# An RWKV block with its MLP on one core: both units of round 0's second part treated together

## The chip, the cores and the metric

The kernel runs on one core of a Trainium2 chip. The core has five engines with instruction queues of their own, which meet only at semaphores: TensorE (PE in the profile; PEld are its weight loads), VectorE (DVE), ScalarE (ACT), GpSimd (POOL) and SyncE (SP, which here only issues DMAs). The metric is the device time of one execution in microseconds (us); lower is better. The kernel before took 469.12 us as the median of 3 runs (468.19 to 469.22).

## The reference

The inputs r, k, v and w have 4 batches, 8 heads, 768 steps and 48 numbers for each head and step; u has 48 for each head. For each batch and head a state of 48 x 48 is carried along the steps, and its result goes through a normalization and a two-layer MLP (384 to 1536 to 384):

```python
for t in range(S):
    cur = np.einsum('bhd,bhe->bhde', u[None] * kt, vt)
    y[:, :, t] = np.einsum('bhd,bhde->bhe', rt, state + cur)
    state = wt[:, :, :, None] * state + np.einsum('bhd,bhe->bhde', kt, vt)
# x: y as (batch, step, head * 48)
xn = (x - mu) / np.sqrt(var + 1e-06) * g_ln
out = x + np.maximum(xn @ w_ch1, 0.0) @ w_ch2
```

## The kernel before, in words

**Rounds, parts and units.** The work is cut into 8 rounds: 4 batches, each in two halves of 384 steps. A round holds all 8 heads, as two units of 4 heads (two pairs each); its 384 steps are three tiles of 128. Round 0 alone is cut further, into a first part of one tile and a second part of two tiles (`parts_of_round`), so that matmuls can begin early.

**One part** (`front`, line 1688). r, k and w are loaded, four steps to a row. Products inside these groups of four are made on VectorE, POOL and ACT (`inner`, tiles `nat_*`, `pad_*`, `rk`, `vals`). PE turns the padded k and r so that steps become columns (`turn`; tiles `k`, `r`, `k_ps`, `r_ps`); `totals` multiplies decays over 4, 8, 16 and 32 steps (`tot`, `decay`). Then come four levels, 2 to 5 (blocks of 4 to 32 steps):

- `quads` (line 806): PE makes the products of r and k between neighbouring blocks, for each unit 16 matmuls per tile of 128 steps (`a<-r,k`; 60, 56, 48 and 32 rows at levels 2, 3, 4 and 5).
- `grow` (line 840): VectorE multiplies k, and then r, in place by the decay of the neighbouring block (`k<-k,tot`, `r<-r,tot`), so that the next level can use them. It must wait for that unit's `quads` of the same level, and the next level's `quads` wait for it.
- `keep` and `keep_last`: masked copies on VectorE (level 4 also as four copies on ACT) and copies on ACT move the products from PSUM into the matrix A.

`inner_by_tile` sends the values inside the groups of four through DRAM into the tile `va`, and `place_own` copies them into A with a mask. `turn_k` turns k back (`kn_ps`). `states` (line 953) makes k times v on PE (`a<-v,k`), and its `scan` on VectorE runs the state through the half tiles: one operation for each pair and step, and, where no state comes from an earlier round, a plain copy for the first (`s<-a`). `inside` multiplies A by v, a tiny POOL operation (`token`) separates it from `outputs`, which adds r times the states (`a<-s,r`). The result is copied into `x`.

**Levels of the second part.** In the second part of round 0 (two tiles) each level's `quads` and `grow` are issued for one unit at a time: the list `apart` in `front` (line 1723) holds two entries, `[0]` and `[1]`. In the first part and in all later rounds it has one entry with both.

**MLP and the rest.** `normalize`, `turn_x`, `first_product` and `mlp` are the normalization and the MLP. Its weights arrive as raw words (`raw`), which ACT, VectorE and POOL make into floats (`convert`: `held`, `rest` with a sign step, a shift `w<-w`, a join `w<-w,held`). Round 0 uses plain fp32 matmuls; from round 1 on the first product uses operands cut into parts.

**What sets the order.** Nothing is left to a scheduler at run time. Every step is given to a `Plan` with a cost, the keys that it reads and writes and the engines that could run it. The method `order` walks through the long hand-out list `ORDER` (line 76), in which a number is a step and a multiple of 10000 on top of it picks the second or third of its engines; so `ORDER` sets the place of each step in its engine's queue, and for many steps the engine. Where the plan's own clock expects PE to wait for more than 0.35 us, `order` also puts in filler matmuls on zeros (`idle<-nought`), in blocks of 128 columns. A POOL operation that shares a port with VectorE is also made to wait for the VectorE operations issued before it.

```python
op = ops[entry % 10000]
e = list(op.costs)[entry // 10000]
```

Of the kernel before, what the change touches and what calls it, by code (L numbers as in the profile page):

```python
# [18 lines left out]
ALU = mybir.AluOpType  # L19
# [44 lines left out]
class Plan:  # L64
# [294 lines left out]
def kernel(  # L359
# [614 lines left out]
    def states(q, part):  # L974
# [25 lines left out]
        def scan():  # L1000
# [23 lines left out]
            count=32 * nc,  # L1024
        )
        plan.add(
            "DVE", 0.01 + 0.174 * NP * len(steps), scan, r=[kv_, (f"decay{rnd}", c0)] + sofar,
            w=[(s_, c0)] + ([last_] if last_ else []), new=[("last", last_)] if last_ else [],
            pri=urgent(part, 22),
        )  # L1030
# [794 lines left out]
```

## Time and profile before

| what | value |
|---|---|
| median of 3 runs | 469.12 us (468.19 to 469.22) |
| the profiled execution, its own time | 468.5 us |
| its span, first to last instruction | 466.7 us |
| PE busy, filler included | 458.0 us (98%) |
| of it filler on zeros | 27.94 us, all in the first 50 us |
| VectorE / ACT / POOL busy | 353.2 / 263.8 / 137.7 us |
| mean granted TensorE clock | 0.998 |

Nearly every instruction is recorded by one helper, so all have line 47; they are told apart by the tiles that they write and read. A row of the instruction list reads: start, duration of the row, engine, operation, output<-inputs, shapes, how often; in brackets the idle time of the engine ahead of it and what ended it. An engine's neighbouring instructions overlap by some hundredths of a microsecond, so the time that one takes from its queue is the distance between two starts. One fp32 matmul of the program shows as two in the trace, since the array takes such operands in two passes.

### The profile page before, as it was taken

How to read it: one execution, taken by the hardware profiler on the slowest of the kernel's cores; microseconds unless marked ns; L12 is line 12 of the kernel's file. 1: busy time of each engine (PE TensorE's matmuls, PEld its weight loads, DVE VectorE, ACT ScalarE, POOL GpSimd, SP SyncE). 2: the span in 40 equal slices, each digit the busy share in tenths (PEclk: the TensorE clock that was granted, in tenths of full speed). 3: DMA queues.
4: the chain of work that ended last, by engine and by line, in shares of the span. 5: the costliest groups of instructions: out<-in, count | busy, mean ns of one | idle time of the engine just before them, and what ended most of it. 6: DMA issues, size and time to landing. Idle time of an engine off the chain costs nothing.

```text
span 466.7 us, 17460 instructions
## 1 busy us (share of the span) xinstructions
PE 458.0 (98%) x7442; PEld 399.7 (86%) x7442; DVE 353.2 (76%) x742; ACT 263.8 (57%) x608; POOL 137.7 (30%) x141
## 2 busy tenths in 40 slices
PE   8999999999999999999999999999999999999996
PEld 5677989766999666989776899999999999999996
DVE  8999999999997768897879887976733535525535
ACT  4697889754765322665621677855555456444440
POOL 4137013332451242353443240221013122321030
PEclk9999999999999999999999999999999999999999
DMA  7987775776658505745630545302222232142011
GB/s 208 277 199 210 205 156 137 233 196 156 174 150 185 111 28 136 166 138 145 157 61 5 86 124 129 111 30 70 84 62 67 76 103 67 37 136 67 35 51 51
DMA packets 105501, 56.23 MB, mean 120 GB/s; under 512 B 61904, under 2 KB 102352, under 8 KB 105424
## 3 DMA queue, kind: packets, MB, share of 16 engines
q1 hardware_dynamic: 105152, 54.92, 45.1%
q8 instruction: 58, 0.95, 0.9%
q10 hardware_dynamic: 272, 0.20, 0.1%
q14 instruction: 19, 0.16, 0.1%
HBM read 45.27 MB, written 7.47 MB: 113 GB/s over the span
## 4 chain that ended last, share of the span: by engine, by line
PE 84%; DVE 10%; POOL 2%; issue 2%; SPq 1%; DMA 1%; DVEq 0%; POOLq 0%
PE h_ps L47 28%; PE a L47 26%; PE o L47 15%; PE o_2P L47 4%; PE o_2D L47 2%; PE k_ps L47 2%; PE r_ps L47 2%; PE kn_ps L47 2%; PE xT_ps L47 2%; DVE nat_k L47 1%; DVE s L47 1%; DVE A L47 1%; SPq L47 1%; DVE vals L47 1%; DMA nat_k<-in_k_dram 1%
## 5 line engine op out<-in xcount | busy, mean ns | idle before, releaser
L47 ACT ACTIVATE h<-h_ps 128x384 f32<-128x384 f32 (+2 forms) x108 | 47.8, 456 | 49.6 <-PE h_ps L47 48.9
L47 PE MATMUL o<-ffn,h 128*128 128x384 f32 x216 | 74.7, 492 | 0.0
L47 DVE SCALAR_TENSOR_TENSOR hD<-hH,hL 128x384 fp32r<-128x384 f32 x60 | 36.3, 616 | 37.1 <-POOL hL L47 16.0
L47 POOL TENSOR_TENSOR hL<-h,hH 128x384 fp32r<-128x384 f32 x28 | 30.1, 1081 | 102.7 <-PE a L47 27.7
L47 ACT ACTIVATE h_ps<-h_ps 128x384 f32<-128x384 f32 x84 | 39.7, 481 | 34.5 <-PE h_ps L47 33.5
L47 PEld LDWEIGHTS o<-ffn,h 128*128 128x128 f32 x216 | 39.2, 190 | 23.1
L47 PEld LDWEIGHTS a<-r,k 48*56 48x56 f32 (+3 forms) x3072 | 39.7, 122 | 10.5 <-issue 4.9
L47 PE MATMUL h_ps<-xd,d 128*128 128x384 f32 x204 | 47.1, 335 | 0.0
L47 PE MATMUL a<-r,k 48*56 48x32 f32 (+3 forms) x3072 | 44.1, 208 | 0.6 <-issue 0.2
L47 PE MATMUL h_ps<-xhl,wl 128*128 128x384 f32 x180 | 40.4, 334 | 0.0
L47 DVE TENSOR_TENSOR r<-r,tot 112x768 f32<-112x768 f32 (+1 forms) x40 | 32.2, 808 | 10.0 <-PE a L47 10.0
L47 PE MATMUL h_ps<-xhl,wh 128*128 128x384 f32 x180 | 39.1, 326 | 0.0
L47 ACT ACTIVATE hH<-h 128x384 fp32r<-128x384 f32 x60 | 29.7, 518 | 11.6 <-PE a L47 7.8
L47 DVE TENSOR_TENSOR k<-k,tot 112x768 f32<-112x768 f32 (+1 forms) x40 | 31.6, 790 | 5.5 <-PE a L47 5.4
L47 PEld LDWEIGHTS h_ps<-xd,d 128*128 128x128 f32 x204 | 34.0, 189 | 0.5
L47 DVE TENSOR_TENSOR hL<-h,hH 128x384 fp32r<-128x384 f32 x32 | 17.9, 568 | 20.0 <-PE a L47 9.5
L47 PEld LDWEIGHTS h_ps<-xhl,wh 128*128 128x128 f32 x180 | 30.8, 189 | 0.0
L47 ACT COPY A<-a 32x384 f32<-32x384 f32 (+5 forms) x56 | 23.5, 421 | 12.4 <-PE a L47 9.8
L47 PEld LDWEIGHTS h_ps<-xhl,wl 128*128 128x128 f32 x180 | 30.1, 189 | 0.2
L47 PE MATMUL a<-w2D,hD 128*128 128x384 f32 x90 | 29.7, 330 | 0.4 <-DVE hD L47 0.4
L47 PE MATMUL idle<-nought 128*128 128x384 f32 (+2 forms) x90 | 27.9, 431 | 0.9 <-DVE eps L47 0.9
L47 ACT ACTIVATE xf<-xT_ps,g_sb 128x384 f32<-128x384 f32 (+2 forms) x27 | 14.7, 549 | 22.1 <-PE xT_ps L47 18.9
(184 smaller groups left out, 1135.3 us busy)
## 6 DMA issues: line engine op xcount, KB each, us to landing
d<-w1d SPq DMA_DIRECT2D x84, 192.0 KB, 2.6
raw<-in_moe_w_ch_dram SPq DMA_DIRECT2D x24, 384.0 KB, 4.0
nat_r<-in_r_dram SPq DMA_DIRECT2D x24, 192.0 KB, 3.8
nat_w<-in_w_dram SPq DMA_DIRECT2D x24, 192.0 KB, 4.1
v<-in_v_dram SPq DMA_DIRECT2D x24, 192.0 KB, 4.2
nat_k<-in_k_dram SPq DMA_DIRECT2D x23, 192.0 KB, 3.9
out_dram<-x SPq DMA_DIRECT2D x15, 192.0 KB, 2.0
w1d<-w1diff SPq DMA_DIRECT2D x12, 192.0 KB, 2.9
```

What stands on the lines that cost most here:

```text
L47: ins = self.tc.keep_in_program_order(f(*args, **kw))
```

## The change

Three things change together.

1. In `front`, the second part of round 0 gives both units to each `quads` and `grow`. For each of four levels there is one group of 32 matmuls where there were two of 16, and one growth of 512 columns for k and one for r where there were two of 256 each. The matmuls are the same.
2. In `scan`, where no state comes from before (the first half of each batch), the first states of both pairs are copied by one operation of 96 columns where there were two of 48. The step's cost in the plan is adjusted.
3. `ORDER` is another list, since the steps are numbered anew; it also gives other places, and for many steps other engines, to the work of all rounds.

```diff
     ORDER = [
-        10008, 3, 4, 10012, 2, 9, 10, 5, 11, 16, 264, 261, 7, 14, 13, 18, 10019, 262, 17, 265, 260, 263,
...
+        2, 10007, 5, 3, 4, 10, 10014, 13, 10012, 9, 11, 16, 18, 17, 19, 261, 260, 265, 262, 263, 15,
...
             for m in steps:
+                if m == 0 and before is None:
+                    DVE.tensor_copy(out=s[:, :, 0, :], in_=kv[:, 0, 0 : NP * TT : TT, :])
+                    continue
                 for pr in pairs:
                     new = kv[:, m % 2, pr * TT + m // 2, :]
                     to = s[:, pr, m, :] if m < 2 * TT - 1 else tiles[last_][0:PD, pr]
-                    if m == 0 and before is None:
-                        DVE.tensor_copy(out=to, in_=new)
-                    else:
-                        c = uu * NM + pr * 2 * TT + m
-                        DVE.scalar_tensor_tensor(
...
+                    c = uu * NM + pr * 2 * TT + m
+                    DVE.scalar_tensor_tensor(
...
         plan.add(
-            "DVE", 0.01 + 0.174 * NP * len(steps), scan, r=[kv_, (f"decay{rnd}", c0)] + sofar,
+            "DVE", 0.01 + 0.174 * (NP * len(steps) - (before is None and c0 == 0)), scan, r=[kv_, (f"decay{rnd}", c0)] + sofar,
...
-        apart = [[uu] for uu in both_units] if rnd == 0 and nc > 1 else [both_units]
+        apart = [both_units]
         for lev in range(LOW, NLEV):
             for us in apart:
                 quads(part, lev, us)
```

In the built program the change of form takes 16 instructions from VectorE (8 growths and 8 copies). The new order brings some others to VectorE: it has 577 entries where there were 588, ACT 582 for 584, POOL 141 for 139 and SP 268 for 269.

More of the change, by code (lines that the diff above doesn't have):

```diff
@@ L1008, in scan @@
                     to = s[:, pr, m, :] if m < 2 * TT - 1 else tiles[last_][0:PD, pr]
-                    if m == 0 and before is None:
-                        DVE.tensor_copy(out=to, in_=new)
-                    else:
-                        c = uu * NM + pr * 2 * TT + m
-                        DVE.scalar_tensor_tensor(
-                            out=to, in0=s[:, pr, m - 1, :] if m else tiles[before][0:PD, pr],
-                            scalar=tiles[f"decay{rnd}"][0:PD, c : c + 1], in1=new,
-                            op0=ALU.mult, op1=ALU.add,
-                        )
+                    c = uu * NM + pr * 2 * TT + m
+                    DVE.scalar_tensor_tensor(
+                        out=to, in0=s[:, pr, m - 1, :] if m else tiles[before][0:PD, pr],
+                        scalar=tiles[f"decay{rnd}"][0:PD, c : c + 1], in1=new,
+                        op0=ALU.mult, op1=ALU.add,
+                    )
         sofar = [before] * (before is not None) if c0 == 0 else [(s_, 0)]
```

256 rows, old and new, of the table ORDER are left out of this document.

## The prediction

> **What bounds the kernel now.** I read the page's busy totals first, then the table of busy time by stage, then the list of instructions of each engine up to 53 us.
>
> ```profile
> span 466.7 us, 17460 instructions
> ...
> PE 458.0 (98%) x7442; PEld 399.7 (86%) x7442; DVE 353.2 (76%) x742; ACT 263.8 (57%) x608; POOL 137.7 (30%) x141
> ```
>
> PE is busy throughout, but this busy time holds filler. The table by stage (its columns: stretch, length, busy PE, weight loads, VectorE, ACT, POOL, granted clock, DMA share, GB/s) and the same for the filler tile alone (PE, weight loads) separate the two:
>
> ```profile
> 10.00:30.00 20.00, 19.02 (x446) 13.65 (x443) 19.66 (x49) 15.44 (x38) 1.54 (x3) 1.00 0.88 241
> 30.00:50.00 20.00, 19.25 (x402) 14.81 (x393) 20.00 (x55) 16.95 (x44) 12.98 (x11) 1.00 0.85 223
> 60.00:100.00 40.00, 40.00 (x689) 32.39 (x682) 39.39 (x89) 33.02 (x82) 11.37 (x11) 1.00 0.77 196
> ```
> ```profile
> 50.00:467.00 417.00, 0.00 (x0) 0.00 (x0) 1.00 0.42 108
> sum 467.00, PE 27.94 PEld 15.95; mean PE 4.66 PEld 2.66
> ```
>
> So there are two regimes. Up to about 49 us VectorE is full (19.66 and 20.00 of 20) and PE burns 27.94 us on filler. After that there is no filler and PE is full with real matmuls at a granted clock of 1.00. PE's real work is the same before and after, so the change is worth what it does to the moment at which PE becomes dense, plus stalls that the new order puts behind it. That moment is the first product of round 1's squares (level 2), 96 matmuls at 49.30, behind round 0's last outputs and one filler:
>
> ```profile
> 20.76 1.00 PE L47 MATMUL a<-r,k 48*48 48x32 f32 x64
> ...
> 45.35 0.49 PE L47 MATMUL idle<-nought 128*128 128x128 f32 x2
> ...
> 49.30 1.57 PE L47 MATMUL a<-r,k 48*60 48x32 f32 x96
> ```
>
> **The VectorE terms.** Here start-to-start counts, since neighbours overlap:
>
> ```profile
> 4.85 0.34 DVE L47 TENSOR_TENSOR rk<-nat_k,nat_r 128x192 f32<-128x192 f32 x1
> ...
> 7.68 0.53 DVE L47 TENSOR_TENSOR pad_k<-pad_k,nat_w 128x192 f32<-128x192 f32 x1 [0.48 <-POOL nat_r L47]
> ...
> 10.44 0.56 DVE L47 TENSOR_TENSOR rk<-nat_k,nat_r 128x384 f32<-128x384 f32 x1 [0.18 <-DVE k L47]
> ...
> 14.40 0.41 DVE L47 TENSOR_TENSOR k<-k,tot 112x256 f32<-112x256 f32 x1
> 14.74 0.41 DVE L47 TENSOR_TENSOR r<-r,tot 112x256 f32<-112x256 f32 x1
> 15.07 0.55 DVE L47 TENSOR_TENSOR pad_r<-pad_r,nat_w 128x384 f32<-128x384 f32 x1
> ...
> 36.62 0.32 DVE L47 COPY s<-a 112x48 f32<-112x48 f32 x2
> 36.86 0.44 DVE L47 SCALAR_TENSOR_TENSOR s<-s,decay,a 112x48 f32<-112x48 f32 x2
> ...
> 44.17 0.64 DVE L47 TENSOR_SCALAR w<-w 128x384 int32<-128x384 int32 x2
> ...
> 51.01 0.96 DVE L47 TENSOR_TENSOR k<-k,tot 112x768 f32<-112x768 f32 x1 [0.64 <-PE a L47]
> 51.88 0.95 DVE L47 TENSOR_TENSOR r<-r,tot 112x768 f32<-112x768 f32 x1
> ```
>
> Growths, merged: 256 columns take 0.335 us of the queue (14.40, 14.74, 15.07), 768 take 0.87 (51.01, 51.88), so 512 take about 0.60, by the straight line between them. Two of 256 take 0.67. Sixteen become eight: 8 x 0.07 = 0.55 us less. A page of the Trainium skill, "VectorE: DVE Perf Modes", section on the fixed extra latency, gives (N+151)/0.96 ns for such an fp32 operation; each merge would then save 157 ns, 1.26 us in all, as an estimate. The single duration agrees (424 ns against 0.41), but the starts show that most of it overlaps with the neighbour, so the trace decides for 0.55.
>
> First states: two copies of 48 take 0.24 (36.62 to 36.86) to 0.31; one of 96 columns costs no less than one of them (0.12) and no more than both. I take 0.17, 0.1 saved per unit, 0.2 in round 0. The six later units (rounds 2, 4, 6) save as much each on an engine that PE hides: nothing.
>
> **What the new order moves in this stretch**, from the built program's lists. Out of the first part's work on VectorE go a copy of k of 512 columns (0.60; to ACT) and three products of 192 at 0.27 (the same line; to POOL), and one of 96 comes back (0.17): 4.93 us of work before the second part's first product (4.85 to 10.44 less 0.48 and 0.18 of idle) become 3.7. That would be over at 8.5. But POOL now stands in front of VectorE's first nat_r product, as it did at 7.68 (0.48 us of wait), and the second part's k is the eighth load of the SP queue instead of the ninth:
>
> ```profile
> 5.50 0.61 SPq L47
> 6.11 0.04 issue
> 6.16 3.50 DMA nat_k<-in_k_dram
> ```
>
> The ninth landed at 9.66 (6.16 + 3.50); one issue of 0.66 (5.50 to 6.16) earlier is 9.0. So the second part starts at 9.0 to 9.7, I take 9.2, instead of 10.44.
>
> From there to the end of the second unit's scan was 33.73 us (44.17 - 10.44). In the new list this stretch holds: growths +0.15 (eight of 0.60 for fourteen of 0.335; before, two more stood behind the scans); copies -0.2; two conversions fewer, -0.54; three small totals to POOL, one decay here, -0.26; nat_w to POOL and a nat_r product back, 0; one more masked copy of 256 (0.34, was four ACT copies); and, fetched from behind the scans, a reduction of 576 (0.67, by the same line), the first statistics (384 columns, 0.47) and a copy of x (0.25). Sum +0.87. The scan ends at 9.2 + 33.73 + 0.87 = 43.8, 0.37 earlier, with 1.4 us less left to do behind it.
>
> **What the merge costs.** Before, one unit's growth covers the other's products. Now a level is a chain: products of both units, 1.00 us (the x64 row at 20.76), a hop, then growths of 1.2. In the new list VectorE has 1.15 us (decay, masked copy, a join) and 1.28 us (masked copy, two growths of the first part) to do between the growths of levels 2, 3 and 4, and 1.9 before level 5. With a hop of 0.1 to 0.15 on either side PE needs 1.2 to 1.3: 0 to 0.15 us of idle per level. So the cover just suffices: 0.15 us in all, which I count. If it fails, 1.0 us per level shows.
>
> *SP's queue.* The loads of the first part's own values stand at places 30, 35 and 37 of SP's list instead of 25, 31 and 34, those of the second part at 36, 39 and 40 instead of 39 to 41. The last of the first part was issued here:
>
> ```profile
> 26.50 0.59 SPq L47 DMA_DIRECT2D va<-own_d  x1
> ```
>
> Three places later, at 0.66, it goes out at 28.5 and is there at 32 to 33 (3.50 as for nat_k, or somewhat more); by the list above the masked copy that needs it comes at 36.1. The cover is 3 us, so this costs nothing; the other loads of weights keep their numbers.
>
> **PE's own list.** Up to round 1's level 2 the real matmuls are the same in number and form, only ordered otherwise. Filler: 96 blocks of 128 columns before, 97 in the head and two more far behind (round 7, levels 4 and 5). At 27.94 / 96 = 0.29 us each the three more cost between nothing (if PE waits there anyway) and 0.9; I take 0.3 for the two late ones, as a block only stands where a gap is expected, and nothing for the head. In the head the last filler is now four blocks, 1.1 us, directly ahead of round 1's squares. From scan to dense took 5.13 us (44.17 to 49.30); the outputs of the two units are now closer, and four blocks replace one there, so I keep 5.1: dense at 48.9.
>
> Sum: -0.4 (head), +0.15 (levels, which the list of VectorE's work leaves out), +0.3 (late gaps), -0.2 (the 1.4 us that no longer stand between the scans and round 1's growths; the growth at 51.01 waited 0.64 for PE, so little of it is on the path) = -0.15, say -0.2. The profiled execution is 468.5 (466.7 and 1.8 around it), 0.6 under the median of 469.12. So 468.3 there, 468.9 as a median: by 0.2% (0.94 us), about what a measurement can tell here, no change.
>
> **Rivals.** *POOL holds the outputs (slower).* POOL now has a sign of a weight row between its last pad_r product and the two tokens that release round 0's last outputs; before, only the product w stood there.
>
> ```profile
> 30.72 5.37 POOL L47 TENSOR_TENSOR decay<-tot 112x8 f32<-112x8 f32 x1 [9.36 <-DVE pad_k L47]
> ...
> 39.40 1.46 POOL L47 TENSOR_TENSOR pad_r<-pad_r,nat_w 128x576 f32<-128x576 f32 x1 [0.21 <-issue]
> ...
> 43.02 0.80 POOL L47 TENSOR_TENSOR w<-nat_w 128x288 f32<-128x288 f32 x1 [0.25 <-DVE last L47]
> 45.11 0.09 POOL L47 MEMSET token<- 1x1 f32 x1 [1.29 <-PE a L47]
> ```
>
> A product of 8 columns took 5.37 there, where the 288 of w took 0.80: VectorE was full beside it (20.00 of 20, growths and products of round 1). The token was not late before (POOL waited 1.29 for PE ahead of it). In the new order pad_k, w and pad_r follow VectorE's nat_r product, which by the list above ends 5.4 us ahead of the last scan, at 38.4; with 1.46, 0.80 and 1.46 the sign starts at 42.1 or later. If it meets the shifts and joins that VectorE runs from 43.8, it can lose as much as the 5.37 us; the tokens are wanted at 45.0 (scan 43.8 and 1.2 for the products inside, 44.17 to 45.35 before). I price it at 2 of the 5 us: 468.9 + 2 = 470.9. It decides once the sign ends after 45. The Trainium skill ("SBUF — State Buffer", "SBUF: two separate sides") says that whoever starts first holds the shared pair for one instruction and the other blocks; by that the sign would lose about one VectorE operation. The 5.37 row disagrees with that as a bound: POOL lost to several in a row.
>
> *The middle loses (slower).* Behind 50 us PE has nothing to gain in the table (40.00 of 40.00), but a new order can lose there: the two late fillers are real stalls with their hops (1.2), and one level of the merged chain shows (1.0), against the head's -0.4: 470.3.
>
> *The head gains fully (faster).* For it speaks that the second part can start at 9.0 and that the 1.4 us fetched ahead of the scans can count in full, in round 1's level 3; against it, the four blocks of filler. Then -0.4 - 0.2 (start) - 0.8 (the rest of the 1.4, less what waits for PE anyway) with nothing lost behind is about -1.4: 467.7.
>
> *The merge does nothing by itself*: VectorE idles exactly what it saves. Then the time is the order's alone; this lies inside the forecast.
>
> **How the numbers follow.** Forecast (within a measurement of 469.1) 0.34, own range 468.2 to 470.0; head gains fully 0.30; middle loses 0.22; POOL holds 0.14. Hence faster 0.30, same 0.34, slower 0.36. The range goes from 467.2 (0.5 under the full gain: merged copies at their good end and the whole 1.4) to 471.2 (the POOL case with its 2 and 0.3 more); longer POOL waits and larger gains are left out, 0.17 in all.
>
> **What would show it.** Right: VectorE as full as before from 10 to 44 us; merged growths near 0.68 long and 0.60 apart; last scan near 43.8; round 1's squares near 48.9; filler near 28.8. Wrong: gaps on VectorE ahead of the growths of levels 3 and 4; a sign on POOL that ends after 45; PE waits of over 0.5 us at the two late fillers.

## The result and the profile after

The changed kernel took 481.7 us (median of four runs, 481.25 to 484.37) against 468.9 us for the kernel before beside it: 1.027 times as long, with a 95% interval of 1.023 to 1.031. The prediction said 468.9 us, in a range of 467.2 to 471.2, so it was wrong: the change costs 2.7%.

The profiled execution after is the slowest of the four, 484.4 us. Its page, with busy totals and the granted clock in 40 slices:

```profile
span 482.6 us, 17401 instructions
...
PE 466.4 (97%) x7440; PEld 405.2 (84%) x7440; DVE 364.0 (75%) x723; ACT 266.5 (55%) x608; POOL 124.6 (26%) x141
...
PEclk9999899999999999999999997999999999999999
```

The span is 15.9 us longer than before (466.7), PE is busy 8.4 us longer with the same real matmuls, and two slices of the clock fall below full speed, where before had none. (The kernel before has longer executions too: 7 of the 53 timed beside the experiments took 473.8 to 476.2 us, at a granted clock of 0.988 to 0.996.) To see where the time goes I worked out a lateness. Each form of matmul gets its mean distance to the next one in the trace of before (behind 50 us), the work still to be done is summed from the end, and the moments at which the two kernels have the same work left are compared:

```
work left, us          410   390   370   350   330   290   230   190   170   110    10
before is there at      52    72    92   112   132   172   233   274   295   354   452
after is late by       5.9   5.9   7.4   7.3   8.3   8.7   8.6   8.7  15.4  14.5  15.8
```

Two large steps carry the lateness: 5.9 us in the head, and 6.7 us between 280 and 310 us. The rest is 1.4 us near 90, 1.0 near 130, 0.4 near 170, and about half a microsecond in the tail.

**The head.** The list of VectorE of the kernel after (start, duration, operation, in brackets its idle time and what ended it):

```profile
6.18 0.36 DVE L47 TENSOR_TENSOR rk<-nat_k,nat_r 128x192 f32<-128x192 f32 x1 [1.16 <-DMA nat_r<-in_r_dram]
...
9.90 0.60 DVE L47 TENSOR_TENSOR pad_k<-nat_k,nat_w 128x384 f32<-128x384 f32 x1
10.96 0.56 DVE L47 TENSOR_TENSOR rk<-nat_k,nat_r 128x384 f32<-128x384 f32 x1 [0.46 <-DMA nat_r<-in_r_dram]
...
20.15 0.69 DVE L47 TENSOR_TENSOR r<-r,tot 112x512 f32<-112x512 f32 x1
20.76 0.68 DVE L47 TENSOR_TENSOR k<-k,tot 112x512 f32<-112x512 f32 x1
...
31.09 0.76 DVE L47 TENSOR_TENSOR rk<-nat_k,nat_r 128x576 f32<-128x576 f32 x1 [1.38 <-DMA nat_r<-in_r_dram]
...
39.91 1.29 DVE L47 COPY_PREDICATED A<-mask_own,va 128x512 f32<-128x512 int8 x1
...
41.93 1.35 DVE L47 TENSOR_REDUCE vals<-nat_r 128x24 f32<-128x1152 f32 x1
43.20 0.25 DVE L47 COPY x<-a 128x96 f32<-128x96 f32 x1
43.37 2.88 DVE L47 COPY_PREDICATED A<-mask_own,va 128x512 f32<-128x512 int8 x1
...
49.05 0.43 DVE L47 SCALAR_TENSOR_TENSOR last<-s,decay,a 112x48 f32<-112x48 f32 x2
...
190.31 1.34 DVE L47 TENSOR_REDUCE vals<-nat_r 128x24 f32<-128x1152 f32 x1
```

The merged growths do what they should (0.61 us apart, 0.69 long). But VectorE waits three times for a load of nat_r, 3.00 us in all, where before had 0.66 us of idle time in the same stretch; and the second masked copy of own values, which took 0.76 us before, takes 2.88. The two masked copies and the last scan in the kernel before, and POOL's row beside the second copy:

```profile
38.48 1.13 DVE L47 COPY_PREDICATED A<-mask_own,va 128x512 f32<-128x512 int8 x1
...
40.76 0.76 DVE L47 COPY_PREDICATED A<-mask_own,va 128x512 f32<-128x512 int8 x1
...
43.83 0.45 DVE L47 SCALAR_TENSOR_TENSOR last<-s,decay,a 112x48 f32<-112x48 f32 x2
```
```profile
40.81 1.95 POOL L47 TENSOR_TENSOR pad_k<-pad_k,nat_w 128x576 f32<-128x576 f32 x1
```

What POOL does in the kernel after:

```profile
41.91 1.42 POOL L47 TENSOR_TENSOR pad_k<-pad_k,nat_w 128x576 f32<-128x576 f32 x1 [1.13 <-DVE nat_r L47]
43.29 0.21 POOL L47 TENSOR_TENSOR decay<-tot 112x16 f32<-112x16 f32 x1
43.47 0.80 POOL L47 TENSOR_TENSOR w<-nat_w 128x288 f32<-128x288 f32 x1
44.22 1.43 POOL L47 TENSOR_TENSOR pad_r<-pad_r,nat_w 128x576 f32<-128x576 f32 x1
48.34 1.64 POOL L47 TENSOR_SCALAR held<-raw 128x384 uint16<-128x384 f32 x1 [2.69 <-DVE s L47]
```

POOL's row of products ends at 45.65 and the copy at 46.25, 0.60 us later. That is about the copy's own time, so it seems to have got next to nothing done until POOL was through with all of them. Before it was the other way round: the copy started 0.05 us ahead of POOL's pad_k and took 0.76 us, and pad_k took 1.95 instead of the 1.42 that it takes at 41.91 here. The last scan now ends near 49.4 instead of 44.2. The 5.2 us that it is later are 2.3 of waits (3.00 less 0.66), 2.3 of the two masked copies (3.95 us of the queue instead of 1.64), and, as the remainder, 0.6 of a longer list.

PE waits for these scans twice and then meets a slower clock (waits in PE's list; then the table by stage, whose last three columns are granted clock, DMA share and GB/s):

```profile
47.67 0.25 PE L47 MATMUL a<-v,A 64*64 64x48 f32 x1 [1.10 <-DVE last L47]
49.53 0.25 PE L47 MATMUL a<-v,A 64*64 64x48 f32 x1 [1.18 <-DVE last L47]
...
55.25 0.97 PE L47 MATMUL a<-r,k 48*60 48x32 f32 x55
```
```profile
50.60:54.00 3.40, 3.40 (x53) 3.00 (x44) 3.40 (x10) 2.93 (x9) 0.00 (x0) 0.51 0.71 204
290.00:294.30 4.30, 4.22 (x164) 3.81 (x156) 4.30 (x8) 3.15 (x7) 1.98 (x3) 1.00 0.78 160
294.30:296.70 2.40, 0.00 (x0) 0.00 (x0) 0.94 (x2) 0.00 (x0) 0.00 (x0) 0.94 0.16 49
296.70:303.00 6.30, 6.28 (x23) 6.01 (x24) 5.36 (x14) 3.45 (x8) 0.00 (x0) 0.50 0.14 37
```

From 50.6 to 54.0 PE is full at half clock, so it does 1.7 us of work in 3.4. Round 1's squares start at 55.25 instead of 49.30.

**The stall near 294 us.** The table shows all engines but VectorE at rest from 294.30 to 296.70, then 6.3 us at half clock. PE's list there:

```profile
292.43 1.02 PE L47 MATMUL a<-r,k 48*32 48x32 f32 x96
293.38 0.90 PE L47 MATMUL a<-s,r 48*64 48x48 f32 x38
296.72 0.45 PE L47 MATMUL a<-s,r 48*64 48x48 f32 x2 [2.44 <-issue]
297.10 1.33 PE L47 MATMUL h_ps<-xhl,wl 128*128 128x384 f32 x3
```

The wait stands between the 38th and the 39th of 40 equal matmuls (counts behind an x are rows of the trace; of the products of r and k the program issues 8 for each unit, tile and level, and the trace has 16 rows for them), whose operands are all there, and nothing in the records released it. In this stretch small matmuls follow each other: level 4, inside, level 5 and the outputs. Instructions come through a queue of their own, in 58 packets of 16 KB over the kernel; the trace has such packets from 285.02, 289.72, 294.50 and 298.08 us on, and the third one runs inside the stall, which ends 1.30 us behind it. That is no chance: the 20 traces of this document hold 36 waits of PE of 0.35 us or more behind 14 us that nothing in the records released, and every one ends 1.29 to 1.54 us behind the end of such a packet. The ends of PE's waits that a record did release lie anywhere from 1.3 to 17.6 us behind one. Behind the stall the clock is halved for 6.83 us, which takes 3.4 us more. 2.44 + 3.4 and two filler blocks that stand there (0.49 and 0.38 us long) give the step of 6.7.

### The profile page after: what moved, and what is told of

Its sections match the earlier page's. It is cut to its first block, busy times and chain, and to the rows that moved or that the text cites. A ratio compares the mean times of both kernels' runs of the same rounds, so it can differ in the third digit from the quotient of the medians.

```text
span 482.6 us, 17401 instructions
## 1 busy us (share of the span) xinstructions
PE 466.4 (97%) x7440; PEld 405.2 (84%) x7440; DVE 364.0 (75%) x723; ACT 266.5 (55%) x608; POOL 124.6 (26%) x141
## 4 chain that ended last, share of the span: by engine, by line
PE 81%; DVE 9%; DMA 5%; SPq 1%; issue 1%; ACT 1%; DVEq 0%
PE h_ps L47 27%; PE a L47 25%; PE o L47 15%; PE o_2P L47 4%; PE o_2D L47 2%; DVE s L47 2%; DVE A L47 2%; DMA nat_r<-in_r_dram 2%; PE r_ps L47 2%; PE xT_ps L47 2%; PE kn_ps L47 2%; PE k_ps L47 2%; SPq L47 1%; DMA d<-w1d 1%; DMA raw<-in_moe_w_ch_dram 1%
## 5 line engine op out<-in xcount | busy, mean ns | idle before, releaser
L47 DVE SCALAR_TENSOR_TENSOR hD<-hH,hL 128x384 fp32r<-128x384 f32 x60 | 37.3, 637 | 34.9 <-POOL hL L47 18.9
L47 POOL TENSOR_TENSOR hL<-h,hH 128x384 fp32r<-128x384 f32 x25 | 26.0, 1048 | 119.7 <-PE o_2P L47 34.1
L47 PE MATMUL h_ps<-xd,d 128*128 128x384 f32 x204 | 48.4, 339 | 0.5 <-DMA d<-w1d 0.5
L47 PE MATMUL h_ps<-xhl,wl 128*128 128x384 f32 x180 | 41.4, 340 | 0.0
L47 DVE TENSOR_TENSOR hL<-h,hH 128x384 fp32r<-128x384 f32 x35 | 23.1, 662 | 23.7 <-ACT hH L47 8.0
L47 PE MATMUL h_ps<-xhl,wh 128*128 128x384 f32 x180 | 40.1, 332 | 0.0
L47 DVE TENSOR_TENSOR r<-r,tot 112x768 f32<-112x768 f32 (+2 forms) x36 | 33.5, 930 | 7.6 <-PE a L47 7.0
L47 DVE TENSOR_TENSOR k<-k,tot 112x768 f32<-112x768 f32 (+2 forms) x36 | 31.0, 863 | 4.7 <-PE a L47 4.6
L47 ACT ACTIVATE xf<-xT_ps,g_sb 128x384 f32<-128x384 f32 (+2 forms) x27 | 14.7, 546 | 28.8 <-PE xT_ps L47 28.7
L47 PE MATMUL idle<-nought 128*128 128x384 f32 (+2 forms) x88 | 29.1, 457 | 0.9 <-DVE eps L47 0.9
L47 ACT COPY A<-a 32x384 f32<-32x384 f32 (+4 forms) x52 | 22.4, 435 | 6.8 <-PE a L47 6.3
```

Source lines behind the costliest of these rows:

```text
L47: ins = self.tc.keep_in_program_order(f(*args, **kw))
```

## The experiments

The numbers in `ORDER` are steps. Where steps differ between the two forms they were renumbered, and nothing else of the method changes. Squares always means the first product of round 1's level 2, where PE becomes dense: 49.30 us before, 55.25 after. Ratios come with their 95% intervals; a range behind a time is the spread of its runs.

**1. The merge alone, in the old order.** The edit takes the merge and the joint copy from the change, and leaves every entry of `ORDER` in its old place and on its old engine; a merged step stands where the first of its two halves stood.

```diff
-        apart = [[uu] for uu in both_units] if rnd == 0 and nc > 1 else [both_units]
+        apart = [both_units]
```

> The two units of round 0's second part are merged and the first-state copies too, but every step keeps the place and engine it had in the order of before (a merged step stands where the first of the two stood). Theory (the new order does the harm): 468 to 471 us, round 1's level-2 squares start at 49 to 50 us, last scan of round 0 near 44. Rival (the merged chain does the harm): 474 us or more, VectorE idle ahead of the merged growths, squares at 53 or later.

Measured: 470.23 us beside 470.15, ratio 0.999 (0.996 to 1.002). Squares at 50.1. So the merge is not what costs 2.7%, and it gains nothing either. One VectorE wait appears, and PE's list shows why:

```profile
28.46 0.69 DVE L47 TENSOR_TENSOR r<-r,tot 112x512 f32<-112x512 f32 x1 [1.24 <-PE a L47]
```
```profile
26.20 0.41 PE L47 MATMUL a<-r,k 48*48 48x32 f32 x17
27.66 0.74 PE L47 MATMUL a<-r,k 48*48 48x32 f32 x47 [1.05 <-issue]
```

The growth was late not because its chain is long but because PE stopped for 1.05 us in the middle of 64 equal matmuls, the same sign as at 294 us in the kernel after.

**2. The new order with the units apart.** Each merged entry of the new list is replaced by its two halves side by side, and the first-state copies are single again.

```diff
-        ... 304, ...
+        ... 305, 307, ...
```

> The order of after with the units apart again (each merged step is replaced by its two halves side by side) and single first-state copies. Theory (order): 480 to 484 us, squares of round 1 at 55 us again. Rival (merge): below 475 us, squares near 50.

Measured: 481.76 us, ratio 1.025 (1.021 to 1.029). Squares at 54.0; the masked copy at 43.66 takes 2.90 us; PE stalls for 2.49 us at 292.91 and runs at half clock for 6.83 us behind it. With the first run this settles the main question: the order does it, with or without the merge.

**3. New head, old rest, and the reverse.** Up to the squares the entries come in one order, behind them in the other.

> After's steps in after's order up to round 1's first squares, everything behind in the order of before. Theory (about 6 us lost in the head, some 2 to a halved clock right behind it, the rest to a stall and a halved clock near 294 us): 475 to 478 us, squares at 55 us, no wait above 1 us behind 100 us. Rival (the head's loss is hidden later, the rest of the order does it): 470 us or less.

> Before's steps and order up to round 1's first squares, everything behind in the order of after. Theory: squares at 49.3 us; the stall near 290 us and the halved clock behind it stay, 474 to 477 us. Rival (the stall near 290 us is a consequence of what the head did to the instruction count or the clock): 468 to 471 us, no wait of PE above 1 us behind 60 us.

Measured: 485.65 us, 1.033 (1.030 to 1.035), and 482.74 us, 1.029 (1.024 to 1.034). The first is spoilt by its seam: behind the new head SP issues a load of raw weights only at 66.69, ACT stands 7.86 us ahead of the conversion that needs it, and PE waits 8.73 us for ACT at 62.75, with the clock halved for 10.24 us behind it. What can be read from it is that the old rest then adds only 0.5 us of lateness over the last 400 us. The reverse, in the table by stage:

```profile
28.00:38.20 10.20, 10.06 (x148) 7.16 (x149) 8.26 (x15) 7.10 (x18) 2.19 (x2) 0.50 0.88 180
```

Here the head of before, with the same list up to the squares, stalled for 1.49 us at 26.66 inside level 4 and then ran 10.2 us at half clock (squares at 54.60). In the profile of before neither happened. So such a stall hangs partly on the single execution, not on the list alone. Behind the squares the new order loses some 9 to 10 us with the old head too (lateness 18.2 at the end, 8.6 soon after the squares): the losses of the rest are not a consequence of the late head. Their size is that of one execution, the slowest of four (486.78 us). Of it 3.4 us lie near 238 us, where the kernel after lost nothing: a row of 192 small matmuls (level 5) ends there, PE stalls for 2.04 us behind it, and the clock is halved for 3.41 us. My expectation of 474 to 477 was too low.

**4. Three cures, one at a time and together.**

*Loads ahead.* Round 0's nine loads in their old order, the product rk ahead of pad_k on VectorE, and the last load of round 1's nat_r ahead of two loads of w (4, 264, 452 are loads of nat_r, 261 and 260 of nat_w, 262 and 263 of nat_k, 5 is u; 9 and 10 are VectorE's products of rk and pad_k).

```diff
-        2, 10007, 5, 3, 4, 10, 10014, 13, 10012, 9,
+        4, 10007, 2, 3, 5, 9, 10, 10014, 13, 10012,
...
-        ... 261, 260, 265, 262, 263, ... 264, ...
+        ... 264, 261, 262, 265, 260, ... 263, ...
```

> After, with nothing changed but the place of loads on SP: round 0's nine loads of r, k, w and u in the order of before (r of the first part first, and rk ahead of pad_k on VectorE), and the last load of round 1's r moved ahead of the two loads of w that stood before it. Theory (3.0 us of the head are three waits of VectorE for nat_r: 1.16, 0.46, 1.38): the waits together under 1 us, last scan of round 0 ends 2 to 3 us earlier (46.5 to 47.5), round 1's squares at 52 to 53.5, total 478 to 480 us. Rival (the waits hide a later bound, POOL or the values through DRAM): squares within 1 us of 55, total 481 to 482.

Measured: 482.46 us (479.12 to 483.89), 1.024 (1.018 to 1.031): nothing gained, squares at 57.6 (in this execution PE also stalled for 1.71 us inside level 4, up to 29.74). The first wait went, and a longer one came at the second part's start:

```profile
11.72 0.56 DVE L47 TENSOR_TENSOR pad_k<-nat_k,nat_w 128x384 f32<-128x384 f32 x1 [1.83 <-issue]
```

The part's nat_k landed 5.5 us after its issue, where before had 3.9. PE had 0.22 us of work from 12 to 14 us and the clock was halved from 15.4 to 18.8. More on this in 6.

*Masked copy ahead.* Entry 323 is the second masked copy of round 0's second part.

```diff
-        ... 472, 323, 215, ...
+        ... 472, 215, ...
...
-        ... 302, 301, 75, ...
+        ... 302, 301, 323, 75, ...
```

> After, with one step of VectorE moved: the second masked copy of the second part's own values stands right behind the first one, ahead of the product nat_r that releases POOL's row of products. Theory (the copy took 2.88 us instead of about 0.7 because it shared the port with POOL's products in a row): the copy takes 0.65 to 0.8, last scan of round 0 ends 1.5 to 2.2 us earlier, total 478.5 to 480 us, less by 1.7 more if the halved clock at 50.6 us goes too. Rival (it waited for its data or its buffer): the copy takes 2 us or more at its new place too, total 481 to 482.

Measured: 477.33 us, 1.014 (1.009 to 1.020), 1.3 points of the 2.7. VectorE's list:

```profile
40.75 0.75 DVE L47 COPY_PREDICATED A<-mask_own,va 128x512 f32<-128x512 int8 x1 [0.59 <-DMA va<-own_d]
...
46.76 0.43 DVE L47 SCALAR_TENSOR_TENSOR last<-s,decay,a 112x48 f32<-112x48 f32 x2
```

The copy takes 0.75 us, the last scan ends 2.3 us earlier, PE's two waits of 1.10 and 1.18 are gone, the clock from 50.6 to 54.0 is 1.00, and the squares come at 51.4. The copy was slow because of its neighbours on POOL. In lateness the head is 2.4 us late instead of 5.9 (5.3 in the second profile of the kernel after, section 6), so about 3 us are the copy's; near 291 us this execution also lost 2.3 us less than the one shown above (a stall of 1.65 us and a clock halved for 3.41), and nothing shows that the copy has to do with that. The Trainium skill ("SBUF — State Buffer", "Who interferes with whom") says that a VectorE instruction with two SBUF inputs contends with a GpSimd instruction that reads SBUF, and that a reduction does not. The traces agree: the masked copies, which read a mask and data, took 2.88 us here and 1.97 and 1.83 us in round 1 (1.09 and 1.03 before) beside POOL's products, and the reduction beside pad_k took 1.35 (41.93), as the same one of a later round did with nothing on POOL beside it (190.31, 1.34). To have POOL beside it is not enough: the copy that started first, before, took 0.76.

*Wide products between.* 997 and 998 (twelve wide matmuls) go ahead of round 7's level 5 (1364), 961 (six wide ones) between it and the outputs (1297).

```diff
-        ... 1678, 1364, 997, 1297, ... 1529, 998, ... 1298, 961, ...
+        ... 1678, 997, 998, 1364, 961, 1297, ... 1529, ... 1298, ...
```

> After, with wide products of the MLP of round 3 moved between the small ones of rounds 6 and 7: twelve ahead of round 7's level 5 and six between it and round 6's last outputs, so that small matmuls no longer stand in one row. Theory (PE ran out of instructions there and the halved clock follows from the stall): no wait of PE above 0.6 us from 280 to 300 us, no halved clock there, total 474.5 to 477 us. Rival (the stall is a wait for data that the records do not show, or it only moves by some matmuls): a wait of 1.5 us or more remains between 285 and 305 us, total 480 us or more. Rival 2 (the halved clock has another cause): the stall goes, the clock is halved all the same, 478 to 480.

Measured: 479.27 us, 1.018 (1.011 to 1.025). The stall falls to 0.76 us (another wait of 0.45 stands behind it), and there is no halved clock anywhere from 54 us to the tail. The step between 280 and 310 us falls from 6.7 to 2.7. The time lies above my 474.5 to 477, since the profiled stretch keeps one of the two fillers and 1.4 us of waits (0.19, 0.76, 0.45).

*All three.*

> The three edits together: loads of r ahead, masked copy ahead, wide products between. Theory (three separate losses that add up): squares of round 1 at 49.5 to 51.5, no halved clock before the tail, total 469.5 to 473 us. Rival (one of them takes the place of another): 474 us or more.

Measured: 478.17 us, 1.017 (1.012 to 1.022), above what was expected of it and no better than the masked copy alone. In the profiled execution pad_k waited 1.56 us for the loads, up to 11.27, and the clock was halved from 15.2 to 18.6 us; it was halved again for 3.41 us from 295.1, behind waits of 0.78 and 0.47 us. So the loads are a part of it.

**5. The parts that were left.**

*The joint first-state copy alone*, on the kernel before, with its own order:

```diff
+                if m == 0 and before is None:
+                    DVE.tensor_copy(out=s[:, :, 0, :], in_=kv[:, 0, 0 : NP * TT : TT, :])
+                    continue
```

> Before with the merged first-state copy alone: one operation of 96 columns for two of 48 in eight units, units apart, order of before. Theory (0.1 us of VectorE for each of round 0's two units, the others hidden behind PE): 468.5 to 470.5 us, ratio 0.998 to 1.001. Rival (any edit to this order costs): 471 us or more.

Measured: 470.70 beside 470.06, ratio 1.000 (0.996 to 1.004). The joint copy lasts 0.25 us, and up to the scans two of them took 0.65 us of the queue here and 0.57 in the kernel after, where the four single ones took 0.55. It saves nothing.

*The reverse of the wide products*: in the kernel before, the outputs and level 5 are moved up against the small matmuls ahead of them, with the wide products behind.

```diff
-        ... 1008, 988, ... 970, ... 1304, 1376, ... 975, ... 1309, ...
+        ... 1008, ... 1304, ... 1376, ... 1305, 1309, 988, 970, 975, ...
```

> The reverse of the wide products between: before, with round 7's level 5 and round 6's last outputs moved into one row with the small matmuls ahead of them (inside, level 5, outputs behind each other, the wide products of round 3's MLP that stood between behind them). Nothing else changes. Theory (small matmuls in a row make PE run out of instructions): a wait of PE of 0.5 to 2.5 us inside one group of equal matmuls between 279 and 290 us, a halved clock behind it if it is above 1.5 us, total 470.5 to 475 us. Rival (the stall of after has another cause): no such wait, 469 to 470 us.

Measured: 474.98 us, 1.011 (1.009 to 1.013). PE's list, and the table by stage:

```profile
280.09 0.51 PE L47 MATMUL a<-r,k 48*48 48x32 f32 x27 [0.51 <-issue]
...
287.72 0.33 PE L47 MATMUL a<-s,r 48*64 48x48 f32 x8 [1.51 <-issue]
```
```profile
288.70:292.10 3.40, 3.40 (x13) 3.40 (x12) 3.10 (x7) 1.44 (x3) 0.62 (x1) 0.50 0.55 117
```

A stall of 1.51 us, again inside the 40 equal outputs, and a halved clock behind it: the kernel before gets the fault of the kernel after when its small matmuls are put in a row. Its lateness jumps there by 5.4 us, of which filler that the method put in ahead of level 5 (282.36, 1.03 us long) is a part. This, the wide products and the place of every such wait behind a packet show the cause of the second step of the result: PE has run out of instructions, and a row of small matmuls uses them up faster than they come.

*Masked copy ahead and wide products together*, with the new order's own loads:

> After with two edits, the masked copy ahead and the wide products between, and its own order of loads. Theory (gains of 4 us and of 2.4 to 4 us add): 472 to 475.5 us, squares of round 1 at 51 to 52 us, the longest wait behind 280 us under 1 us. Rival (the second only gains when the head is late): 476.5 us or more.

Measured: 477.14 us (475.47 to 481.54), 1.018 (1.012 to 1.024). The profiled execution (477.4) ran at a clock of 1.00 up to its tail, with squares at 51.5, and still a stall of 0.97 and a wait of 0.45 near 293. The gains do not add. Near 293 us this execution lost 3.0 us where the one with the masked copy alone lost 4.4, but it had lost 1.8 us more before that (0.8 near 135 us and 1.1 near 205, the latter with a wait of 0.44 for v). The second profile of the kernel after loses 1.3 near 205 too and the first 0.5, so it changes from execution to execution; why was not found.

*More filler instructions* on the merge in the old order: the same filler time in matmuls of 128 columns.

```diff
...
-                    count += 4 * -(-n // 3)
+                    count += 4 * n
...
-            now = min(n, TT)
+            now = min(n, 1)
...
```

> The merged units in the order of before, with the same filler time cut into matmuls of 128 columns instead of up to 384, so that PE passes through some 200 more instructions in the head and reaches each later matmul at another count. Theory (the wait of 1.05 us inside level 4 at 26.6 us, which held VectorE for 1.24 us, hangs on where the fetched pieces of instructions end): that wait goes or stands at another group, last scan of round 0 within 0.3 us of 44, total 468.5 to 470.5 us, or as much slower as a new wait says. Rival (the wait is for data): it stays where it was, 1 us long, total as with the merged units before, 470.2.

Measured: 472.46 us (469.48 to 477.57), 1.004 (1.002 to 1.006). The stall at 26.6 is gone (level 4 runs its 64 matmuls in one piece, 26.73, 0.92 us), the last scan starts at 43.92 and the squares at 49.4. In exchange PE stops elsewhere:

```profile
296.78 0.59 PE L47 MATMUL h_ps<-xhl,wh 128*128 128x384 f32 x2 [1.40 <-issue]
```

That fits stalls which hang on where the 16 KB pieces end. It is not shown by this run, since one execution of each was profiled and the same program can have such a stall in one execution and not in another (the kernel after has none in level 4 in its first profile and one of 0.74 us in its second).

**6. What was still open: the loads, and the wait near 88 us.**

> The kernel of the run with the loads ahead, profiled a second time. If the late landing of the second part's nat_k (5.5 us behind its issue, where 3.8 to 4.0 is usual) came from this order of loads, it lands 5 us or more behind its issue again and the second part's first product starts at 11.5 or later. If it came from that execution, it lands after 3.8 to 4.2 us, the product starts at 9.9 to 10.4, and the squares of round 1 come at 53 to 55.5 us.

> After, unchanged, profiled a second time, to see which of its losses stay. Theory: the masked copy (2.8 to 3.0 us) and the stall of PE near 290 to 295 us (1 to 2.8 us) stay; the wait for round 1's nat_r at 31 us, which two kernels with the same loads in front of it did not show, may go; squares of round 1 at 53.5 to 56, total 480 to 484. Rival (all three waits for nat_r belong to the order): 1.1 to 1.4, 0.4 to 0.5 and 1.0 to 1.4 us again.

Measured: the one execution of the loads ahead took 484.27 us and pad_k again waited (1.37 us, at 11.14), so three executions with that order of loads showed it (1.83, 1.56, 1.37). After took 481.58 us, 1.023 (1.017 to 1.029), and its second profile shows what stays:

```profile
6.48 0.36 DVE L47 TENSOR_TENSOR rk<-nat_k,nat_r 128x192 f32<-128x192 f32 x1 [1.46 <-DMA nat_r<-in_r_dram]
11.03 0.56 DVE L47 TENSOR_TENSOR rk<-nat_k,nat_r 128x384 f32<-128x384 f32 x1 [0.24 <-DVE pad_k L47]
...
32.10 1.36 DVE L47 TENSOR_TENSOR nat_k<-nat_k,nat_r 128x1152 f32<-128x1152 f32 x1 [0.15 <-ACT pad_k L47]
...
42.73 2.90 DVE L47 COPY_PREDICATED A<-mask_own,va 128x512 f32<-128x512 int8 x1
```

The first wait for nat_r, the masked copy and PE's stall (2.80 us at 293.07) are of the order. The wait of 1.38 us for round 1's nat_r was of that one execution.

Up to its eleventh DMA the SP list of the loads ahead differs from that of before in one thing: a second load of raw MLP weights follows at once. Set back behind v and g (entries 65 and 0 ahead of 110), alone and with the two other cures:

```diff
-        ... 268, 110, ... 42, 65, ... 312, 0, ...
+        ... 268, 65, 0, 110, ... 42, ... 312, ...
```

> The loads ahead once more, and the second load of raw MLP weights, which the new order put right behind the first one at 7.4 us, set back behind v and g as in before, so that SP's first thirteen DMAs are those of before. Theory (the raw weights shared the DMA engines with the part's last load of k and made it land 1.4 to 1.8 us late, twice): second part's pad_k without the wait of 1.37 to 1.83 us, at 9.9 to 10.4, no halved clock in the head before 45 us, squares of round 1 at 53 to 54.5 us (52 if the masked copy alone is left), total 479 to 481. Rival (the late landing has another cause): pad_k at 11 us or later again, total 482 to 484.

> The same with the masked copy ahead and the wide products between. Theory: 0.5 to 1.5 us below masked and wide (477.1), 475.6 to 476.6, squares of round 1 at 50 to 51. Rival: 478.2 as with the three edits together.

Measured: 481.28 us, 1.027 (1.022 to 1.031), and 476.53 us, 1.014 (1.012 to 1.016). The pad_k wait falls to 0.85 and 0.65 us, so the raw load was part of it; the rest of the late landing is not explained. The squares of the first come at 53.3, 2 us earlier than after, but its last scan ends only 0.45 us earlier: the clock was not halved behind the two waits for the scans in this execution, which is worth 1.7. The total of the first does not gain, since its execution had a stall of 2.63 us and 6.83 us of halved clock near 291; that of the second had 6.83 us of halved clock in its head, behind a stall of 1.61 us inside level 4.

For the wait near 88 us, round 1's two masked copies (495, 496) were put next to each other ahead of the reduction that releases POOL's products (664), with the masked copy ahead and the wide products between; then two loads were moved on top (nat_r ahead of u, and 452).

```diff
-        ... 520, 664, ... 189, 496, ... 254, 495, ...
+        ... 520, ... 496, 495, 664, ... 189, ... 254, ...
```

> Masked copy ahead and wide products between, as before, and the same cure in round 1: its two masked copies of own values stand next to each other ahead of the reduction that releases POOL's products w, pad_r and pad_k of round 2. Theory (the two copies of 768 columns took 1.97 and 1.83 us instead of 1.03 to 1.09 beside POOL, and PE's wait of 1.0 us at 84.5 to 88 us for the scan comes from it): copies of 1.0 to 1.1 us, PE's wait under 0.3 us, total 1.0 to 1.5 us below masked and wide, 475.5 to 476.5. Rival (the scan is late for another reason): the wait stays at 0.7 us or more, total 477.

> The three edits of masked both rounds and wide, and two loads moved: the first part's nat_r issued ahead of u, and the last load of round 1's nat_r two places earlier. Theory (the first wait for nat_r, 1.16 to 1.37 us, falls by one issue, 0.65): first product of rk at 5.5 to 5.7 us, squares of round 1 at 50.5 to 51.2, total 0.5 to 1 us less than without. Rival (the landing of the loads is set by what the queues carry, not by their order): nothing gained, or a half clock in the head as in the run with the loads ahead.

Measured: 477.61 us, 1.015 (1.009 to 1.021), and 476.35 us, 1.012 (1.005 to 1.019). The copies (VectorE) and PE's waits with four edits:

```profile
5.23 0.73 DVE L47 TENSOR_TENSOR rk<-nat_k,nat_r 128x192 f32<-128x192 f32 x1 [0.16 <-DMA nat_r<-in_r_dram]
...
75.31 1.93 DVE L47 COPY_PREDICATED A<-mask_own,va 128x768 f32<-128x768 int8 x2 [1.07 <-DMA va<-own_d]
```
```profile
79.55 0.43 PE L47 MATMUL r_ps<-ident,pad_r 128*112 128x128 f32 x2 [1.35 <-POOL pad_r L47]
```

Two copies now take 1.93 us where they took 3.80, so in round 1 it was the same sharing. But the gain went into a new wait: VectorE now waits 1.07 us for the copies' data, POOL's pad_r comes later, and PE waits 1.35 us for that at 78.2, behind a new filler of 1.05 us, instead of 1.0 for the scan at 88. Moving nat_r ahead of u does shorten the first wait: between 1.12 and 1.58 us in the executions with nat_r behind u, it is 0.16. The squares come at 51.2, but they came at 51.5 with the masked copy ahead and wide products alone, and the intervals of the totals overlap. (The three edits without the loads had the clock halved for 3.41 us in the head, from 27.35.)

With all that, 476.4 us is the best that the new order reached here, 1.2% above before. Of its lateness of 8.0 us in the profiled execution 2.3 lie in the head, 2.3 near 80 us, 2.5 near 293 us, and 0.9 behind. No version beat the kernel before.

## Why the prediction was wrong, step by step

Two steps failed. The masked copies were moved at their old duration, with nothing for it in the sum, and the second took 2.88 us instead of 0.76 beside POOL's products. And the stretch behind 50 us was priced at 0.3 us of late gaps, where the profiled execution lost 10 (lateness 5.9 to 15.8), most of it in one stall of PE and the halved clock behind it.

**The frame.** VectorE full in the head and PE full behind it was read rightly, and so was the number of real matmuls. Wrong was to use the sentence that PE has nothing to gain behind 50 us as if it had little to lose there. A queue without gaps at full clock is a state that the old order holds in most executions and the new one does not: 2.44 us of stall and 5.1 us of work lost to halved clocks (half of 3.41 and of 6.83) stand in no term of my sum, and they are nearly half of the loss of the profiled execution.

**The merged growths** (0.60 apart, 0.68 long): right, 0.61 and 0.69. (Eight of 0.60 less fourteen of 0.335 are 0.11 us, not the 0.15 of the sum; nothing hangs on it.) **The first states** (0.2 us saved in round 0): mis-sized, nothing saved (0.57 for 0.55).

**The merged chain** (0 to 0.15 us of idle per level): right for the kernel after, whose levels show no wait of VectorE for PE in the first profile. Where a level did wait, 1.24 us in the old order, it was PE's stall and not the chain.

**The start of the second part** (9.2 instead of 10.44): wrong. Its pad_k starts at 9.90 and rk at 10.96. I followed the place of nat_k in SP's queue and not that of nat_r. The first part's nat_r had gone behind w and u, 1.16 us of wait, and the run with four edits, where the first wait is 0.16, shows that this place was the cause. The second wait, 0.46, was 0.24 in another execution; the third, 1.38, was not of the order.

**VectorE's list** (1.23 us shorter in the first part, 0.87 longer behind): mis-sized. Leaving out the waits and the masked copies it came out 0.6 us longer than before, not 0.36 shorter.

**The masked copies** were costed at their duration in the old trace, moved or not. This is the term of the head that failed most dearly: 2.3 us of VectorE, and with the halved clock behind it about 3 us of lateness in the head. The total fell by 4 to 6 us without it (from 1.027 or 1.023 to 1.014), but what goes beyond these 3 us is not shown to be the copy's; 2.3 us of it, in the profiled execution, lie near 291 us. The row that could have warned me was quoted, POOL's decay of 5.37 us beside a full VectorE; I drew from it that POOL can lose and not that VectorE can.

**The own values' cover** (3 us, so nothing): held, no copy waited for its data in the kernel after. But it was thin for the second part: moved up right behind the first one, the copy had to wait for its data (0.59 us, there at 40.75).

**The late fillers** (0.3 us): 0.49 and 0.38 us long (filler in all 29.1 us, 28.8 expected), and they did not cover the stall that followed. **From scan to dense** (5.1 us): 5.85 with the halved clock in it, 4.3 with the masked copy ahead.

**The rivals.** *POOL holds the outputs* saw the right two engines and the wrong direction. The sign started only at 48.34, released by the scan, so it held nobody; the products ahead of it held VectorE. That its price of 2 us is near the 2.1 that the copy lost is luck. *The middle loses* had the right sign and ended 11 us too low (its own terms, 1.2 and 1.0 less 0.4, make 470.9 on the median of 469.1, and its 470.3 only on the profiled execution): it priced late fillers and one level, and had neither the stall's 2.4 us nor the clock in it. *The head gains fully* fell with the scan end, 49.4 against 43.8. *The merge does nothing by itself* was true, and I used it to say that the order alone decides; it did, but the forecast had priced the order by moving old durations about.

**What stays open.** Why a load of nat_k lands 1.4 to 1.8 us later behind the loads in the old order was only partly found. Why stalls of 0.4 to 1.6 us come inside round 0's level 4 in some executions and not in others (before has none, the same head had one of 1.49) was not tried; that PE waited for instructions there too is shown by the packets. Nor is it known how much of each total such stalls make, since one or two executions of each kernel were profiled. The waits near 130 us (0.55 us for w1d) were not tried either.

## What to carry to other kernels

A list of moves can't be costed by the durations that its operations had elsewhere: for each operation that is moved, look which operation of the engine that shares its port will stand beside it, and count the slower case too. Where PE is dense, a new order can only lose, so look in its list for rows of small matmuls (here some 280 in 6 us, with one group of wide ones between) and for waits close together, and price them with the halved clock that can follow. And if an order is retuned together with a change of form, run the form in the old order first: it would have shown in one run that the form was worth nothing here.

## What the runs showed of the hardware

*PE can run out of instructions.* Waits of 0.4 to 2.8 us stood inside or right behind groups of equal matmuls, released by nothing, and all 36 of them ended 1.29 to 1.54 us behind the end of a 16 KB packet of the instruction queue. One of 1.51 us came when small matmuls were put in a row, and one of 2.44 shrank to 0.76 when wide ones were put between. The Trainium skill ("Runtime: NRT & Kernel Launch", "Instruction fetch mechanics") says that instructions come in blocks of 16 KiB, which the packets of this case agree with, and that the cost of crossing one is mostly hidden, which these stalls contradict.

*The halved clock goes by a grid.* All halved stretches before the tail lasted 3.41, 6.83 or 10.24 us, and in every run the stretches of full clock between them are whole multiples of 3.413 us. It followed the pair of waits of 1.10 and 1.18 us, 0.7 us apart, in six of the eight executions that had this pair, and, behind 10 us, single waits of 1.49 to 2.80 us, in one execution a single wait of 1.00 us (the clock halved from 27.35) and in one a pair of 0.78 and 0.47. But single waits of 1.70 and 1.71 us and a pair of 0.97 and 0.45 did not bring it, so where a wait lies in the grid seems to count; that is not shown. The page "TensorE: Matmul & The Clock Gate" of the Trainium skill, in its part on the clock gate, has a free-running window of 3413 ns, with which this agrees, and gives an idle window as the condition; here waits well short of one were enough.

*POOL can win a row of handovers.* One masked copy ended 0.60 us behind the last of the POOL products that ran beside it (2.88 us, and 2.90 in the second profile). So it gave way to the one that ran when it started and to two that started after it. In the kernel before the same copy, started 0.05 us ahead of a POOL product, took 0.76.
